# An mLSTM attention, a two-expert mixture and a dense layer in one kernel: where the steps of experts 0 and 1 stand, and when the second batch is routed

## The chip, the cores and the metric

One core of a Trainium2 chip. The metric is the device time of one execution in microseconds (us), the median over runs. The engines are TensorE (PE, matmuls; PEld is its weight loads), VectorE (DVE), ScalarE (ACT), GpSimd (POOL) and SyncE (SP, here the queue that issues most DMAs). Each engine takes its instructions in the order of the program; semaphores tie them together.

## The reference

Three layers follow each other. The attention is a recurrence over 768 tokens for 2 batches and 8 heads of 40; its output x (1536 tokens of 320 values) is routed to 2 of 8 experts, and the mixture's output goes through a dense layer with g = h cos h.

```python
h_tilde = np.einsum('bhde,bhe->bhd', C, qt)          # C, n: running states of the attention
y[:, :, t] = o * h_tilde / np.maximum(np.abs(nq), 1.0)
...
noisy_logits = x @ w_gate + np.log1p(np.exp(x @ w_noise)) * noise
top2 = np.argpartition(-noisy_logits, 2, axis=1)[:, :2]
...
h = np.maximum(x[mask] @ w1[e], 0.0)
out[mask] += top2_w[mask, k, None] * (h @ w2[e])
...
h = x @ w_in
return (h * np.cos(h)) @ w_out
```

## The kernel before

**Attention.** The recurrence is worked in chunks of 128 tokens, 6 per batch, so chunks n = 0 to 11; `att_step(n)` issues one. A chunk has its scores (`mm_s`), decay weights on ACT and POOL (`mk_w`), the product of both on DVE (`mk_p`, tile ppt), the scaled queries (`mk_q`, tile qtt, on POOL or DVE by a list of n), the running state (`mm_state`, `mk_state`, tile st), the output matmuls (`mm_out`, L306 and L310, tile pS) and the normalized rows (`mk_y`: an Abs on ACT, L321, and four DVE instructions, L322 to L327, that end in xt, called x(n) here). x(n) is written to DRAM (xd) by SP, transposed on PE (`rt_a`, L346), copied on ACT (L348), multiplied with the gating weights (`rt_b`, L355) and copied again (L359, tile Lt).

**Routing.** When a batch's six chunks are done, `router_a0` to `router_d` turn the gate values into lists of token indices: three small ACT instructions, then DVE work from L398 to L519 with two small products on PE (`router_b`, L441 to L444, and `router_c`, L504). `gather` (L546, on POOL) then fetches the rows of x of one group from DRAM into xgt.

**Experts.** Ten groups are worked: experts 0 and 1 on batch 0 (groups 0 and 1, up to 240 tokens each), experts 2 to 7 on both batches (up to 448), and experts 0 and 1 on batch 1. Each group has 8 steps of 128 hidden units; step k is step k mod 8 of group k // 8. Before its first step the gathered rows are transposed on PE and split on ACT and DVE into a high and a low part (`prep_slot`: L555, L557, L558, tiles xh and xl). `expert_step` first issues `split(k + 2)`, which cuts the weights of a later step into wh (a copy on ACT, L585) and wl (a subtraction, L587, on POOL, or on DVE in the two-slot groups for the k that L586 names), then the first product `mm1` (L594, 8 matmuls into pS), a Relu on ACT (L646, hb) and the low part on DVE (L649), and last the second product of the step before (`mm2`, L599 to L603, 6 matmuls into pA). The third matmul of mm1 is the first that reads wl. In this kernel steps of groups 0 and 1 have odd wl on DVE but for k in `POOL_SPLIT`, and 12 and 14 too.

**Order.** It is written out by hand. `manual_schedule` keeps the order in which the Python code issues, on each engine. Tables hold what is issued at which place: `mid[n]` and `fill[n]` inside `att_step(n)`, `put(n, ...)` behind it; after the attention the same `put(k, ...)` counts expert steps. `K0` is the first step of the main loop. Before, steps 0 to 3 are issued within chunks 10 and 11 and step 4 behind chunk 11; the second batch's routing then goes on behind steps 5 to 12, and the gathers of group 2 behind steps 10 and 11. From step 71 on the dense layer's steps follow (`moe2_step`), while its weights are converted on DVE between.

Of the kernel before, what the change touches and what calls it, by code (L numbers as in the profile page):

```python
# [15 lines left out]
OP = mybir.AluOpType  # L16
# [5 lines left out]
NC = S // C  # L22
# [18 lines left out]
def tile_mlstm_moe_moe2(ctx, tc, qk, kv, og, gi, gf, wcat, noise, wm1, wm2, cst, out):  # L41
    nc = tc.nc
    V, A, G, T, Y = nc.vector, nc.scalar, nc.gpsimd, nc.tensor, nc.sync
# [188 lines left out]
    def mk_q(n):  # L232
        if n >= 2 * NC or n % NC == 0:
            return
        d = L[n]
        d["qt"] = ap_.tile([128, NH, C], FT, name="qtt", bufs=2)
        (G if n in (1, 4, 5, 6, 7, 8, 9, 11) else V).tensor_tensor(out=d["qt"], in0=d["qk"][:, 2], in1=d["ge"], op=OP.mult)

    def mm_s(n, ws=range(NH)):
        if n >= 2 * NC:  # L240
            return
        d = L[n]
        for i in ws:
# [55 lines left out]
    def mm_out(n, between=None):  # L299
        c = n % NC  # L300
        d = L[n]
        p = d["po"] = psS()
        so = STS[(n + 1) % 2]
        for w in range(NH):
            if c:
                T.matmul(p[:, 82 * w:82 * w + 82], d["qt"][:, w, :], so[:, w, :], start=True, stop=False,  # L306
                         skip_group_check=True)
            for s in range(2):
                h = 2 * w + s
                T.matmul(twice(p, h), d["p"][:, h, :], d["v"][:, h:h + 1, :].to_broadcast([128, 2, 41]),  # L310
                         start=(not c), stop=bool(s) or not c, skip_group_check=True)
            if between and w < NH - 2:
                between(w)
# [221 lines left out]
    groups = [(e, T2, 2 * e) for e in (0, 1)]  # L535
# [37 lines left out]
        prep_x(d["xg"][i], groups[g][1][i], d["xh"], d["xl"], 128 * i, ps_)  # L573

    SP = {}
    POOL_SPLIT = (1, 7, 9, 11, 65, 67, 75)

    def split(k):
        g, f = divmod(k, 8)
        if g >= NG:  # L580
            return
        raw = WB[groups[g][0]]
        wh = mp.tile([128, FW], FR, name="wh", tag="wh", bufs=4)
        wl = mp.tile([128, FW], FR, name="wl", tag="wl", bufs=4)
        A.activation(wh, raw[:, f, :], AF.Copy)  # L585
        eng = V if len(groups[g][1]) == 2 and (k % 2 and k not in POOL_SPLIT or k in (12, 14)) else G  # L586
        eng.tensor_tensor(out=wl, in0=raw[:, f, :], in1=wh.bitcast(FT), op=OP.subtract)  # L587
        SP[k] = (wh, wl)

# [264 lines left out]
    def att_step(n):  # L854
        if n == 0:
            loads(0)
        if n:
            mk_e(n + 1)
        for f, a in pre.pop(n, []):
            f(*a)  # L860
        mm_state(n)
        if n:
            mm_s(n + 2, (0,))
        mm_out(n, (lambda w: mm_s(n + 2, (w + 1,))) if n else None)
        if n == 0:
            gates_t(2, 4)
        if n:
            rt_a(n - 1, psS if n == 7 else None)
        mm_s(n + 2, (3,) if n else range(NH))
        for f, a in mid.pop(n, []):  # L870
            f(*a)
        if n:
            rt_b(n - 1, psS if n == 9 else None)
        if n == 2:
            gates_t(4, NC)
        mk_state(n)
        mk_p(n + 1)
        mk_q(n + 1)
        mk_decay(n + 1)
        if n == 0:  # L880
            gates_c(2, 4)
        if n == 2:
            gates_c(4, NC)
        if n == 1:
            gates_a(4, NC)
        loads(n + 1)
        if n == 2 * NC - 1:
            mk_y(n)
        for f, a in fill.pop(n, []):
            f(*a)  # L890
        if n < 2 * NC - 1:
            mk_y(n)
        mk_w(n + 2)
        if n == 0:
            V.tensor_copy(tri, cc_[:, 0:128])
            V.tensor_copy(rb[:, 0], row0)
            V.memset(ones, 1.0)
            V.memset(os_[:, NC], 0.0)
        if n == 1:
            gates_b(4, NC)  # L900
        if n == 10:
# [15 lines left out]
    for i in range(8):  # L917
        put((6, 7, 8, 8, 8, 9, 9, 9)[i], load_w, 0, i, 1)
    put(10, load_w, 1, 0, 2)
    put(11, load_w, 1, 2, 2)  # L920
    put(11, load_w, 1, 4, 2)
    mid[6] = [(A.preload_act_table_set, ("natural_log_exp_and_others",))]
    fill[6] = [(router_a0, (0,))]
    put(6, router_a1, 0)
# [3 lines left out]
    fill[8] = [(router_b1, (0, 0))]  # L928
    put(8, router_b1, 0, 1)
    put(8, router_s)  # L930
    put(9, split, 1)
    mid[9] = [(router_c, (0,))]
    fill[9] = [(router_d, (0,)), (gather, (0, 0)), (gather, (0, 1)), (split, (0,))]
    put(9, router_a3, 0)
    put(10, router_a4, 0)
    mid[10] = [(prep_slot, (0, 0, psA)), (prep_slot, (0, 1, psA))]
    fill[10] = [(step, (0,))]
    put(10, step, 1)
    mid[11] = [(step, (2,))]
    put(11, step, 3)  # L940
    for i in range(2):
        put(10, gather, 1, i)
    K0 = 5
    for n in range(2 * NC):
        att_step(n)
        for f, a in at.pop(n, []):
            f(*a)
    rt_a(2 * NC - 1)
    step(4)
    rt_b(2 * NC - 1)  # L950
    router_a0(1)
    router_a1(1)
    att.close()
    wp = ctx.enter_context(tc.tile_pool(name="wp", bufs=1, reuse_waits="tile"))

    put(5, load_w, 1, 6, 2)
    put(5, router_a2, 1)
    put(5, prep_slot, 1, 0, psA)
    put(6, prep_slot, 1, 1, psA)
    put(6, router_b, 1)  # L960
    put(7, router_b1, 1, 0)
    put(7, router_b1, 1, 1)
    put(8, router_b2, 1)
    put(9, router_p, 1)
    put(10, router_c, 1)
    put(10, router_d, 1)
    put(11, router_a3, 1)
    put(12, router_a4, 1)
    for i in range(4):
        put(10 + i // 2, gather, 2, i)  # L970
        put((13, 14, 15, 15)[i], prep_slot, 2, i, (psA, psM)[i % 2])
    for g in range(2, NG - 1):
        n = len(groups[g + 1][1])
        for i in range(n):
# [20 lines left out]
    for f in range(12):  # L995
        k = 18 + (15 * f) // 4
# [166 lines left out]
```

## Time and profile before

| | |
|---|---|
| device time, three runs | 522.0, 523.95, 525.42 us (median 523.95) |
| span of the profiled execution, first to last instruction | 520.4 us |
| PE busy in the span | 489.0 us, 94% |
| PE weight loads, DVE, ACT, POOL busy | 468.5, 368.6, 326.0, 274.5 us |
| chain that ended last | PE 74%, DVE 13%, ACT 4%, DMA 4%, issue 3% |

The page gives no other time of the profiled execution than its span. The profile's lists of instructions in order of time ("timeline") give, for one engine, start, duration, line, operation and tiles; in brackets stands how long the engine was idle before, and what released it. "x3" is three instructions merged. The lists by stretch ("windows") give an engine's busy time within a part of the span. Times in the text are microseconds from the span's start.

### The profile page before, as it was taken

Reading aid. Unit: us, or ns where it says so; the run is one execution under the profiler, and the core shown is the slowest. Engines: PE = TensorE matmul, PEld = TensorE weight load, DVE = VectorE, ACT = ScalarE, POOL = GpSimd, SP = SyncE. Lnnn points to the kernel's source line nnn. Section 1 sums busy time; section 2 is a strip of 40 time slices with the busy share of each in tenths; the row PEclk is TensorE's granted clock in tenths of the full one; section 3 lists DMA queues with packets and bytes.
Section 4 is the critical chain, followed back from the end, with each engine's and each line's share of the span. In section 5 each row is a group of like instructions: output and inputs, shape, how many; then the busy total and the mean of one; then the engine's idle time right before and its main releaser. Section 6 shows DMA issues by size and latency. Waiting matters only on the chain.

```text
span 520.4 us, 9011 instructions
## 1 busy us (share of the span) xinstructions
PE 489.0 (94%) x3198; PEld 468.5 (90%) x3198; DVE 368.6 (71%) x779; ACT 326.0 (63%) x695; POOL 274.5 (53%) x234
## 2 busy tenths in 40 slices
PE   4899997799999999999999997999999999999995
PEld 3788886799999999999999997899999999999995
DVE  8874496568468776878776678788956655687773
ACT  3657866356555455545455475578877777777773
POOL 6435466556856868595868687264356347300000
PEclk9999999799999999999999999999999999999999
DMA  6889885386373918291938284130021003001001
GB/s 185 240 268 268 269 282 174 111 287 242 114 286 115 349 65 298 110 362 39 348 130 274 97 332 145 33 112 14 1 64 52 1 1 102 13 2 38 1 2 43
DMA packets 25396, 76.36 MB, mean 147 GB/s; under 512 B 3872, under 2 KB 11392, under 8 KB 25344
## 3 DMA queue, kind: packets, MB, share of 16 engines
q1 hardware_dynamic: 22752, 67.11, 37.2%
q0 software_dynamic: 2592, 8.61, 5.6%
q8 instruction: 27, 0.44, 0.3%
q14 instruction: 25, 0.20, 0.1%
HBM read 66.47 MB, written 9.22 MB: 145 GB/s over the span
## 4 chain that ended last, share of the span: by engine, by line
PE 74%; DVE 13%; ACT 4%; DMA 4%; issue 3%; SPq 0%; POOL 0%; DVEq 0%; ACTq 0%; POOLq 0%
PE pS L594 34%; PE pA L603 10%; PE pA L600 10%; PE pA L599 10%; PE pM L555 2%; PE pS L310 1%; PE pA L612 1%; PE pA L611 1%; ACT wt L209 1%; DMA xgt<-xd,idxe 1%; PE pM L355 1%; DMA gb<-gd 1%; DVE c_t L717 1%; DVE ppt L256 1%; DVE r_am L483 1%
## 5 line engine op out<-in xcount | busy, mean ns | idle before, releaser
L587 POOL TENSOR_TENSOR wl<-wraw,wh 128x704 fp32r<-128x704 f32 x69 | 122.9, 1790 | 61.6 <-ACT wh L585 55.7
L649 DVE SCALAR_TENSOR_TENSOR hb<-pS,hb 128x384 fp32r<-128x384 f32 (+2 forms) x128 | 45.9, 390 | 45.6 <-ACT hb L646 44.9
L585 ACT ACTIVATE wh<-wraw 128x704 fp32r<-128x704 f32 x80 | 62.9, 786 | 14.3 <-PE pA L611 7.3
L594 PE MATMUL pS<-xh,wh 128*128 128x448 f32 (+1 forms) x240 | 69.9, 346 | 0.5 <-ACT xh L557 0.5
L594 PE MATMUL pS<-xh,w 128*128 128x384 f32 x288 | 66.7, 340 | 1.6 <-DVE m_t L758 1.6
L594 PE MATMUL pS<-xh,wl 128*128 128x448 f32 (+1 forms) x240 | 66.5, 332 | 0.4 <-POOL wl L587 0.4
L599 PE MATMUL pA<-wh,hb 128*128 128x320 f32 x208 | 62.3, 309 | 0.0
L600 PE MATMUL pA<-wl,hb 128*128 128x320 f32 x208 | 62.2, 309 | 0.0
L743 ACT ACTIVATE m_t<-pS,magic 128x384 f32<-128x384 f32 x64 | 37.0, 579 | 28.7 <-PE pS L594 23.8
L646 ACT ACTIVATE hb<-pS 128x448 fp32r<-128x448 f32 (+1 forms) x80 | 37.7, 471 | 26.2 <-PE pS L594 18.5
L594 PEld LDWEIGHTS pS<-xh,w 128*128 128x128 f32 x288 | 50.0, 188 | 2.9 <-DVE m_t L758 2.9
L758 DVE SCALAR_TENSOR_TENSOR m_t<-m_t,pS 128x384 f32<-128x384 f32 x64 | 35.4, 553 | 16.7 <-ACT m_t L757 14.6
L603 PE MATMUL pA<-wh,hb 128*128 128x320 f32 x208 | 44.1, 312 | 3.0 <-DVE hb L649 2.9
L594 PEld LDWEIGHTS pS<-xh,wl 128*128 128x128 f32 x240 | 43.5, 192 | 2.7 <-POOL wl L587 0.5
L594 PEld LDWEIGHTS pS<-xh,wh 128*128 128x128 f32 x240 | 41.1, 192 | 1.5 <-ACT xh L557 0.6
L744 DVE TENSOR_SCALAR m_t<-m_t 128x384 f32<-128x384 f32 x64 | 23.1, 360 | 27.3 <-ACT m_t L743 27.0
L764 POOL TENSOR_TENSOR wl<-m_t,wh 128x384 fp32r<-128x384 f32 x25 | 25.4, 1016 | 30.7 <-ACT wh L762 21.4
L594 PE MATMUL pS<-xl,wh 128*128 128x448 f32 (+1 forms) x160 | 39.7, 329 | 0.0
L600 PEld LDWEIGHTS pA<-wl,hb 128*128 128x128 f32 x208 | 38.7, 186 | 0.6
L599 PEld LDWEIGHTS pA<-wh,hb 128*128 128x128 f32 x208 | 38.6, 186 | 0.6
L546 POOL DMA_INDIRECT xgt<-xd,idx x28 | 34.4, 1228 | 7.8 <-DVE idx L519 3.2
L745 DVE SCALAR_TENSOR_TENSOR m_t<-pS,m_t 128x384 f32<-128x384 f32 x64 | 35.7, 558 | 2.2
(201 smaller groups left out, 1239.7 us busy)
## 6 DMA issues: line engine op xcount, KB each, us to landing
wraw<-wm SPq DMA_DIRECT2D x36, 704.0 KB
raw<-wm SPq DMA_DIRECT2D x16, 704.0 KB
qk<-qk SPq DMA_DIRECT2D x24, 240.0 KB
gb<-gd SPq DMA_DIRECT2D x10, 512.0 KB
kv<-kv SPq DMA_DIRECT2D x12, 324.0 KB
yd<-yt SPq DMA_DIRECT2D x22, 160.0 KB
wraw<-wm SPq DMA_DIRECT2D x8, 352.0 KB
ogt<-og SPq DMA_DIRECT2D x6, 320.0 KB
```

Of the source, the lines that this page charges most:

```text
L546: G.indirect_dma_start(out=t[:n, :], out_offset=None, in_=XD[0:S, :] if g < 2 else XD[:, :], in_offset=bass.IndirectOffsetOnAxis(ap=(idxe ...
L585: A.activation(wh, raw[:, f, :], AF.Copy)
L587: eng.tensor_tensor(out=wl, in0=raw[:, f, :], in1=wh.bitcast(FT), op=OP.subtract)
L594: T.matmul(p[:, :n], w[:, 128 * k:128 * k + 128], x[:, m, :], start=(i == 0), stop=(i == 7))
L599: T.matmul(a[:n, :DM], hh[:, s], wh[:, KW:], start=first, stop=False)
L600: T.matmul(a[:n, :DM], hh[:, s], wl[:, KW:], start=False, stop=False)
L603: T.matmul(a[:n, :DM], hl[:, s], wh[:, KW:], start=False, stop=last)
L646: A.activation(hh[:, :n], p[:, :n], AF.Relu)
L649: V.scalar_tensor_tensor(out=hb[:, o:o + z - a], in0=p[:, a:z], scalar=0.0, in1=hh[:, a:z].bitcast(FT), op0=OP.max, op1=OP.subtract)
L743: A.activation(t, m["p"], AF.Identity, bias=magic, scale=0.5 / PI)
L745: V.scalar_tensor_tensor(out=t, in0=m["p"], scalar=0.5 / PI, in1=t, op0=OP.mult, op1=OP.subtract)
L758: V.scalar_tensor_tensor(out=s, in0=s, scalar=1.0, in1=m["p"], op0=OP.subtract, op1=OP.mult)
```

## The change

Steps 0 to 3 and the transposes of group 0 (`prep_slot`) are no longer issued within chunks 10 and 11. The two transposes stand at the end of chunk 11, steps 0 and 1 behind it, and the main loop starts with step 2. Splits 0 and 1 are issued behind chunk 10. In chunk 10, `mk_y` stands ahead of the next chunk's `mk_q` and `mk_p`, and the transposes of x(10) stand ahead of chunk 11's output matmuls. qtt of chunk 11 is made on DVE. Among the splits, 12 and 14 are POOL's again and 3 too, while 9 and 11 become DVE's. The second batch's routing is spread over steps 0 to 7 and not 4 to 10, and the gathers of group 2 stand behind steps 7 and 8, not 10 and 11. The last load of expert 1 is issued behind chunk 11.

```diff
--- before.py
+++ after.py
@@ -234,7 +234,7 @@
             return
         d = L[n]
         d["qt"] = ap_.tile([128, NH, C], FT, name="qtt", bufs=2)
-        (G if n in (1, 4, 5, 6, 7, 8, 9, 11) else V).tensor_tensor(out=d["qt"], in0=d["qk"][:, 2], in1=d["ge"], op=OP.mult)
+        (G if n in (1, 4, 5, 6, 7, 8, 9) else V).tensor_tensor(out=d["qt"], in0=d["qk"][:, 2], in1=d["ge"], op=OP.mult)
 
     def mm_s(n, ws=range(NH)):
         if n >= 2 * NC:
@@ -573,7 +573,7 @@
         prep_x(d["xg"][i], groups[g][1][i], d["xh"], d["xl"], 128 * i, ps_)
 
     SP = {}
-    POOL_SPLIT = (1, 7, 9, 11, 65, 67, 75)
+    POOL_SPLIT = (1, 3, 7, 65, 67, 75)
 
     def split(k):
         g, f = divmod(k, 8)
@@ -583,7 +583,7 @@
         wh = mp.tile([128, FW], FR, name="wh", tag="wh", bufs=4)
         wl = mp.tile([128, FW], FR, name="wl", tag="wl", bufs=4)
         A.activation(wh, raw[:, f, :], AF.Copy)
-        eng = V if len(groups[g][1]) == 2 and (k % 2 and k not in POOL_SPLIT or k in (12, 14)) else G
+        eng = V if len(groups[g][1]) == 2 and k % 2 and k not in POOL_SPLIT else G
         eng.tensor_tensor(out=wl, in0=raw[:, f, :], in1=wh.bitcast(FT), op=OP.subtract)
         SP[k] = (wh, wl)
 
@@ -861,10 +861,12 @@
         mm_state(n)
         if n:
             mm_s(n + 2, (0,))
+        if n == 2 * NC - 1:
+            rt_a(n - 1)
         mm_out(n, (lambda w: mm_s(n + 2, (w + 1,))) if n else None)
         if n == 0:
             gates_t(2, 4)
-        if n:
+        if 0 < n < 2 * NC - 1:
             rt_a(n - 1, psS if n == 7 else None)
         mm_s(n + 2, (3,) if n else range(NH))
         for f, a in mid.pop(n, []):
@@ -874,8 +876,13 @@
         if n == 2:
             gates_t(4, NC)
         mk_state(n)
-        mk_p(n + 1)
-        mk_q(n + 1)
+        if n == 2 * NC - 2:
+            mk_y(n)
+            mk_q(n + 1)
+            mk_p(n + 1)
+        else:
+            mk_p(n + 1)
+            mk_q(n + 1)
         mk_decay(n + 1)
         if n == 0:
             gates_c(2, 4)
@@ -888,7 +895,7 @@
             mk_y(n)
         for f, a in fill.pop(n, []):
             f(*a)
-        if n < 2 * NC - 1:
+        if n < 2 * NC - 2:
             mk_y(n)
         mk_w(n + 2)
         if n == 0:
@@ -917,8 +924,8 @@
     for i in range(8):
         put((6, 7, 8, 8, 8, 9, 9, 9)[i], load_w, 0, i, 1)
     put(10, load_w, 1, 0, 2)
-    put(11, load_w, 1, 2, 2)
-    put(11, load_w, 1, 4, 2)
+    for i in (2, 4, 6):
+        put(11, load_w, 1, i, 2)
     mid[6] = [(A.preload_act_table_set, ("natural_log_exp_and_others",))]
     fill[6] = [(router_a0, (0,))]
     put(6, router_a1, 0)
@@ -928,47 +935,44 @@
     fill[8] = [(router_b1, (0, 0))]
     put(8, router_b1, 0, 1)
     put(8, router_s)
-    put(9, split, 1)
     mid[9] = [(router_c, (0,))]
-    fill[9] = [(router_d, (0,)), (gather, (0, 0)), (gather, (0, 1)), (split, (0,))]
+    fill[9] = [(router_d, (0,)), (gather, (0, 0)), (gather, (0, 1))]
     put(9, router_a3, 0)
     put(10, router_a4, 0)
-    mid[10] = [(prep_slot, (0, 0, psA)), (prep_slot, (0, 1, psA))]
-    fill[10] = [(step, (0,))]
-    put(10, step, 1)
-    mid[11] = [(step, (2,))]
-    put(11, step, 3)
+    put(10, split, 0)
+    put(10, split, 1)
+    fill[11] = [(prep_slot, (0, 0, psA)), (prep_slot, (0, 1, psA))]
     for i in range(2):
-        put(10, gather, 1, i)
-    K0 = 5
+        put(11, gather, 1, i)
+    K0 = 2
     for n in range(2 * NC):
         att_step(n)
         for f, a in at.pop(n, []):
             f(*a)
     rt_a(2 * NC - 1)
-    step(4)
+    step(0)
     rt_b(2 * NC - 1)
     router_a0(1)
     router_a1(1)
+    step(1)
     att.close()
     wp = ctx.enter_context(tc.tile_pool(name="wp", bufs=1, reuse_waits="tile"))
 
-    put(5, load_w, 1, 6, 2)
-    put(5, router_a2, 1)
+    put(2, router_a2, 1)
+    put(3, router_b, 1)
+    put(4, router_b1, 1, 0)
+    put(5, router_b1, 1, 1)
     put(5, prep_slot, 1, 0, psA)
+    put(6, router_b2, 1)
     put(6, prep_slot, 1, 1, psA)
-    put(6, router_b, 1)
-    put(7, router_b1, 1, 0)
-    put(7, router_b1, 1, 1)
-    put(8, router_b2, 1)
-    put(9, router_p, 1)
-    put(10, router_c, 1)
-    put(10, router_d, 1)
-    put(11, router_a3, 1)
-    put(12, router_a4, 1)
+    put(7, router_p, 1)
+    put(7, router_c, 1)
+    put(7, router_d, 1)
+    put(9, router_a3, 1)
+    put(10, router_a4, 1)
     for i in range(4):
-        put(10 + i // 2, gather, 2, i)
-        put((13, 14, 15, 15)[i], prep_slot, 2, i, (psA, psM)[i % 2])
+        put(7 + i // 2, gather, 2, i)
+        put((12, 13, 14, 14)[i], prep_slot, 2, i, (psA, psM)[i % 2])
     for g in range(2, NG - 1):
         n = len(groups[g + 1][1])
         for i in range(n):
```

On PE, around chunk 11, the end of chunk 10's output matmuls, x(9)'s transposes and what follows them. Tiles: st and qtt feed the state's part of the output, ppt and kv the chunk's own part; xgt are gathered rows, wc the gating weights. Before:

```order
L310 MATMUL pS<-kv,ppt 128x82
L346 MATMUL pM<-ident,xt 128x128 x3
L555 MATMUL pA<-ident,xgt 128x128 x3
L555 MATMUL pA<-ident,xgt 128x112 x3
L355 MATMUL pM<-wc,xTt 128x128 x3
L594 MATMUL pS<-xh,wh 128x240 x2
L594 MATMUL pS<-xh,wl 128x240 x2
L594 MATMUL pS<-xl,wh 128x240 x2
```

and now:

```order
L310 MATMUL pS<-kv,ppt 128x82
L346 MATMUL pM<-ident,xt 128x128 x3
L355 MATMUL pM<-wc,xTt 128x128 x3
L346 MATMUL pM<-ident,xt 128x128 x3
L306 MATMUL pS<-st_99,qtt 128x82
L310 MATMUL pS<-kv,ppt 128x2x41 x2
L306 MATMUL pS<-st_99,qtt 128x82
L310 MATMUL pS<-kv,ppt 128x2x41 x2
```

The transposes of the gathered rows and the two steps behind them have left this place; chunk 11's output follows x(10)'s transposes directly.

On DVE, the same place in the change, from the last state update to chunk 11's products (den is the denominator, ogt the output gate):

```order
L293 TENSOR_TENSOR st_99<-pS,st_99 40x4x41 x2
L322 TENSOR_SCALAR den<-den 128x8
L323 RECIPROCAL den<-den 128x8
L324 SCALAR_TENSOR_TENSOR ogt<-ogt,den 128x320
L327 SCALAR_TENSOR_TENSOR xt<-pS,ogt 128x320
L237 TENSOR_TENSOR qtt<-qk_93,get 128x512
L256 TENSOR_TENSOR ppt<-pA,wt 128x512 x2
```

and before, from there to the products and x(10):

```order
L558 TENSOR_TENSOR xl<-pA,xh 128x2x112
L560 TENSOR_TENSOR xh<-pA,xh 64x112
L293 TENSOR_TENSOR st_99<-pS,st_99 40x4x41 x2
L256 TENSOR_TENSOR ppt<-pA,wt 128x512 x2
L649 SCALAR_TENSOR_TENSOR hb<-pS,hb 128x240
L322 TENSOR_SCALAR den<-den 128x8
```

x(10) has moved ahead of chunk 11's products, and qtt has come from POOL to stand between.

On POOL, at the gathers of group 2 (xgt<-xd,idx), with the splits (wl) around them. Before, the splits for steps 9, 10 and 11 (their names end in 1406, 1433 and 1465), four gathers, and the split for step 16 (1622):

```order
L587 TENSOR_TENSOR wl_1406<-wraw_1150,wh_1405 128x704
L587 TENSOR_TENSOR wl_1433<-wraw_1150,wh_1432 128x704
L587 TENSOR_TENSOR wl_1465<-wraw_1150,wh_1464 128x704
L546 DMA xgt_1532<-xd_103,idx_113 128x320
L546 DMA xgt_1534<-xd_103,idx_113 128x320
L546 DMA xgt_1561<-xd_103,idx_113 128x320
L546 DMA xgt_1563<-xd_103,idx_113 64x320
L587 TENSOR_TENSOR wl_1622<-wraw_1402,wh_1621 128x704
```

and now, from the splits for steps 7 and 8 (1345, 1377) over 10 and 12 (1463, 1522) to 14 (1569):

```order
L587 TENSOR_TENSOR wl_1345<-wraw_761,wh_1344 128x704
L587 TENSOR_TENSOR wl_1377<-wraw_1110,wh_1376 128x704
L546 DMA xgt_1456<-xd_103,idx_113 128x320
L546 DMA xgt_1458<-xd_103,idx_113 128x320
L587 TENSOR_TENSOR wl_1463<-wraw_1110,wh_1462 128x704
L546 DMA xgt_1490<-xd_103,idx_113 128x320
L546 DMA xgt_1492<-xd_103,idx_113 64x320
L587 TENSOR_TENSOR wl_1522<-wraw_1110,wh_1521 128x704
L587 TENSOR_TENSOR wl_1569<-wraw_1110,wh_1568 128x704
```

The splits for steps 10 and 12 have come to stand behind gathers that wait for the second batch's indices.

## Rows read from the trace of the kernel before

**Rows 1.** Windows: stretch, its length, busy of each engine, clock, DMA share, GB/s

```profile
80.00:100.00 20.00, 13.80 (x107) 12.90 (x106) 11.50 (x31) 10.02 (x26) 12.29 (x13) 0.83 0.43 142
...
120.00:140.00 20.00, 19.26 (x145) 17.95 (x144) 13.63 (x39) 11.58 (x24) 13.64 (x10) 1.00 0.37 127
140.00:160.00 20.00, 20.00 (x122) 19.08 (x121) 13.33 (x23) 10.73 (x18) 12.45 (x10) 1.00 0.74 275
```

**Rows 2.** Timeline of PE, chunk 10's output and the gathered rows

```profile
84.94 0.42 PE L306 MATMUL pS<-st,qtt 128*128 128x82 f32 x2 [0.76 <-DVE r_hi L513]
...
87.65 0.49 PE L346 MATMUL pM<-ident,xt 128*128 128x128 f32 x3
90.18 0.55 PE L555 MATMUL pA<-ident,xgt 128*128 128x128 f32 x3 [2.04 <-DMA xgt<-xd,idxe]
93.92 0.82 PE L555 MATMUL pA<-ident,xgt 112*128 112x112 f32 x3 [3.19 <-DMA xgt<-xd,idxe]
```

**Rows 3.** Windows of 2 us, columns as in rows 1; the third last is the clock

```profile
90.00:92.00 2.00, 0.55 (x3) 0.31 (x3) 0.70 (x2) 0.49 (x1) 2.00 (x4) 0.90 1.04 408
92.00:94.00 2.00, 0.08 (x1) 0.09 (x2) 0.02 (x1) 0.00 (x0) 2.00 (x2) 0.50 0.23 89
...
98.00:100.00 2.00, 2.00 (x16) 2.00 (x16) 1.71 (x5) 1.27 (x4) 1.84 (x2) 0.89 0.03 8
```

**Rows 4.** Timeline of DVE, chunk products, x(9), x(11), and the routing's ends

```profile
82.90 1.29 DVE L256 TENSOR_TENSOR ppt<-pA,wt 128x512 f32<-128x512 f32 x2
84.11 0.68 DVE L237 TENSOR_TENSOR qtt<-qk,get 128x512 f32<-128x512 f32 x1
...
85.23 0.16 DVE L322 TENSOR_SCALAR den<-den 128x8 f32<-128x8 f32 x1
...
86.19 0.49 DVE L327 SCALAR_TENSOR_TENSOR xt<-pS,ogt 128x320 f32<-128x320 f32 x1
...
107.19 0.49 DVE L327 SCALAR_TENSOR_TENSOR xt<-pS,ogt 128x320 f32<-128x320 f32 x1
...
111.75 0.21 DVE L398 SCALAR_TENSOR_TENSOR pM<-Lt,pM 128x48 f32<-128x48 f32 x1 [1.50 <-ACT pM L393]
...
124.59 0.18 DVE L519 TENSOR_SCALAR idx<-r_hi 128x32 uint32<-128x32 f32 x1
```

**Rows 5.** Timeline of PE, x(11)'s transposes and step 16's first matmul

```profile
107.83 0.52 PE L346 MATMUL pM<-ident,xt 128*128 128x128 f32 x3 [0.71 <-DVE xt L327]
...
134.50 0.68 PE L594 MATMUL pS<-xh,wh 128*128 128x448 f32 x2 [0.47 <-ACT xh L557]
```

**Rows 6.** Timeline of ACT, an earlier chunk's copy of x and its Abs

```profile
74.94 0.49 ACT L348 ACTIVATE xTt<-pM 128x384 f32<-128x384 f32 x1 [1.83 <-PE pM L346]
...
76.53 0.17 ACT L321 ACTIVATE den<-pS 128x8 f32<-128x8 f32 x1
```

**Rows 7.** Timeline of POOL, first and last gather of group 2, a later split

```profile
125.05 1.37 POOL L546 DMA_INDIRECT xgt<-xd,idx  x1 [3.19 <-DVE idx L519]
...
129.22 0.99 POOL L546 DMA_INDIRECT xgt<-xd,idx  x1 [0.30 <-PE pA L600]
...
138.40 1.71 POOL L587 TENSOR_TENSOR wl<-wraw,wh 128x704 fp32r<-128x704 f32 x1 [0.36 <-ACT wh L585]
```

**Rows 8.** Line 587 on DVE (min, median, max ns); timelines of POOL and DVE

```profile
L587 DVE TENSOR_TENSOR wl<-wraw,wh x11: 877/884/1498, 100.6 to 327.3; 128x704 fp32r<-128x704 f32 x11
...
326.37 1.72 POOL L587 TENSOR_TENSOR wl<-wraw,wh 128x704 fp32r<-128x704 f32 x1 [3.48 <-ACT wh L585]
...
327.34 1.50 DVE L587 TENSOR_TENSOR wl<-wraw,wh 128x704 fp32r<-128x704 f32 x1 [0.34 <-ACT wh L585]
```

**Rows 9.** Chain of waits, 84 to 136 us: start, length, what

```profile
96.05 2.99 PE pS L594 x16
...
125.61 0.90 PE pS L594 x8
...
127.38 0.90 PE pS L594 x8
```

## The prediction

> **What bounds the kernel now.** I read the busy time by stretches first. From 140 us TensorE (PE) is busy 20.00 of 20 us, and from 120 to 140 us 19.26 of 20; the gap is in 80:100, where it is busy 13.80 us at a mean granted clock of 0.83 [rows 1]. So only what lies between about 84 us and the first step of the third group (step 16, whose first matmul starts at 134.50 [rows 5]) can become shorter; right behind it PE is full, and whatever step 16 gains or loses, the end gains or loses. I measure the change by the time at which step 16 starts.
>
> PE's own timeline then shows what the gap is. Chunk 10's output matmuls run from 84.94 us, the transposes of x(9) end at 88.14, and then PE stands before the two transposes of gathered rows (L555), first 2.04 us, then 3.19 us, for the gather [rows 2]. They stand in PE's row ahead of everything left of the attention. The clock falls from 2.4 GHz late in 90:92 (mean 0.90), is at 0.50, its lower level of 1.2 GHz, in 92:94, and is back by 98:100 (mean 0.89) [rows 3]. Sixteen matmuls of two steps took 2.99 us there, where eight take 0.90 us at full clock [rows 9].
>
> Last I read the other three engines. The last chunk's x(11), from which the second batch's routing starts, is ready on VectorE (DVE) at 107.19 + 0.49 = 107.68 us. The routing chain starts on DVE at 111.75 (L398) and ends with the indices at 124.59 + 0.18 = 124.77 us (L519) [rows 4]: 13.02 us, with hardly an idle moment on DVE between. GpSimd (POOL) starts the four gathers of group 2 at 125.05 and ends them at 130.21, 1.29 us each; a split of weights takes it 1.7 us [rows 7].
>
> **The change, part by part.** *Attention.* Steps 0 to 3 and the two transposes leave PE's row ahead of chunk 11; the gather is hidden behind the chunk. What is left there is one chain through three engines, with PE waiting. From 88.14: from the start of x(9)'s copy on ScalarE (ACT) to the end of the next denominator's Abs is 74.94 to 76.70, 1.76 us [rows 6], so 90.0 with a small hand-over. Denominator to x takes 85.23 to 86.68, 1.45 us [rows 4]: x(10) at 91.45. Its product qtt(11), moved from POOL to DVE, takes 0.68 us and the two ppt 1.29 us [rows 4].
>
> Now the hidden price of moving it. The splits 0 and 1 on POOL (1.7 us each [rows 7]) now stand at the same moment: the first begins about 90.8 and ends about 92.5. In the trace a DVE instruction with both inputs in SBUF that meets such a split doesn't run beside it: DVE's split at 327.34 took 1.50 us where the median of the 11 is 0.88, and ended 0.75 us after POOL's of 326.37 to 328.09 [rows 8]. qtt at 84.11 met nothing. The Trainium skill, "SBUF — State Buffer", section "SBUF: two separate sides", states this as a rule: a GpSimd operation and a VectorE one with two SBUF inputs exclude each other for a whole instruction. By it qtt(11) waits for the split; by qtt's own row it costs 0.68 us and x(11) comes 1.1 us earlier. I take the wait, because of rows 8: qtt(11) ends at 93.25, the first ppt at 93.9, and chunk 11's output matmuls, 84.94 to 87.65 or 2.71 us [rows 2], of which the first 0.2 need only qtt, end at 96.4. A gating product, copy and Abs (1.2 us) and 1.45 us for x follow: x(11) at 99.1, 8.6 us earlier than before.
>
> *PE behind x(11).* Steps 0 to 3 must now be done here. A plain step is 1.77 us, 0.90 of it the first product (mm1), 0.87 the second (mm2) [rows 9]. Before, four mm1 and three mm2 were done by 107.83, when x(11) was transposed [rows 5]: 4 x 0.90 + 3 x 0.87 = 6.2 us come in. The waits around the last two transposes of group 2, about 1.3 us of the time ahead of 134.50, go, since these stand a step earlier now. Of the 26.67 us from 107.83 to 134.50, 12 mm1 and 12 mm2 are 21.24; the other 5.4 are routing products, transposes and waits, and without the 1.3 us some 4 us of small work, the same work at other places in the change. Without any other wait step 16 would start at 134.5 - 8.6 + 6.2 - 1.3 = 130.8 us; counted up from 99.1 with 16 mm1, 15 mm2 and 4 us of small work it is 130.6. I take 130.5: a gain of 4.0 us.
>
> *Routing and POOL.* This gain is lost again. L398 starts 4.07 us after x(11) before; one mm1 stands between now instead of a whole step, so 102.3. The 13.02 us on DVE held one split of weights, now it is two, those for steps 5 and 9 (0.9 us more [rows 8]); the copy of a result, 0.4 us, goes behind. Steps of 1.77 us pace the parts, which I price at 1.1 us of short waits, plus 0.5 us for a DVE split meeting POOL's: an estimate from rows 8 and 9. Indices at about 102.3 + 15.1 = 117.4. That is bounded below by 13.0 (115.3) and above by 17 (119.3).
>
> Before, the split for step 10 was done ahead of the gathers on POOL, and 12 and 14 were DVE's. Now POOL's row is two gathers, split 10, two gathers, split 12. In order on one engine: 117.4 + 0.28 + 2 x 1.29 + 0.36 + 1.7 [rows 7] = 122.3 for split 10. PE wants it at 99.3 + 2.4 (small work) + 10 x 0.90 + 9 x 0.87 + 0.2 = 118.7, two matmuls into mm1 of step 10. It waits 3.6 us. Everything of PE stands behind it. Then 2 x 1.29 + 0.15 + 0.36 + 1.7 = 4.8 us later, at 127.1, split 12; PE gets there 3.5 us after its restart, at 125.8, and waits 1.3 us more. These two waits, 4.9 us, take all of the gain.
>
> *What is hidden.* The loads of experts 1 and 2 are issued in the same order on SP, and the DMA engines are busy for 0.43 and 0.37 of 80:100 and 120:140 [rows 1]. The early splits 0 and 1 are wanted only at 99.8, ready by 95. Gathers of group 1 land some 10 us before use. SP's longer wait for x(11) is over earlier than before. Nothing there is on the path; if a load were late, it would cost at most its own 2 or 3 us.
>
> **Sum.** 130.5 + 4.9 = 135.4, against 134.5: +0.9 us, bounded by -4.0 (POOL in time) and about +3 (indices at 119.3). The span would be 521.3. The page's span is 520.4; the median of the runs, 523.95, lies 3.55 us above it, and I let that stay. So 523.95 + 0.9, rounded to 525.0 us: no change that a measurement of this kernel could tell, which needs about 1% (5.2 us).
>
> **The rivals.** *POOL in time.* If the routing on DVE runs with less waiting than I priced, or PE is later at step 10 for other reasons, the 4.9 us go. For it: before, PE waited only for tenths between 108 and 133 us although DVE was full. Against it: step 7's end alone fixes the last routing product at about 114.5, and two gathers and a split need 4.9 us more, so split 10 can't be there before 119.8. Even then about 1.1 us is lost. Time: 523.95 - 4.0 + 0.5 = 520.5, at the very best 519.5. Chance 0.16.
>
> *The clock falls in the attention's tail* (the slower side). Before, it fell late in 90:92, after PE had worked 0.55 us since 88.14, and rose in 98:100, with PE at work since 93.92 [rows 2, 3]. Now PE does about 0.9 us between 88.1 and 91.5 and then waits again until 93.9. If the clock falls there, chunk 11's output, the gating product and mm1 of step 0 take 2.99/1.80 = 1.66 times their time [rows 9]: (2.5 + 0.65 + 0.9) x 0.66 = 2.7 us, all on the chain to x(11) and from it: 525.0 + 2.7 = 527.7. If it falls again in the wait of 3.6 us at step 10, some 0.9 us more remain after the wait at step 12: 528.6; with late indices 530. The Trainium skill, "TensorE: Matmul & The Clock Gate", section "What's actually happening", says that the slow state is the default and activity releases it, which speaks for this rival; it decides if the clock falls ahead of chunk 11's matmuls. Chance 0.28.
>
> *DVE becomes the bound.* Seven steps' worth of routing, splits and results on one engine: if each meeting with a POOL split costs 0.75 us as in rows 8, and three or four occur, the indices come at 119.3 and step 16 at 137.3: 526.8. For it: rows 8. Against: most such pairs fall apart in time. Chance 0.11.
>
> **How the numbers follow.** Forecast 0.45 (its own range 523.5 to 526.5), rivals 0.16, 0.28, 0.11. The range 520.5 to 529.8 takes in the lower half of the first rival and nearly all of the second. Faster by over 1% (below 518.7) needs more than the first rival's best: 0.04. Slower by over 1% (above 529.2) needs the clock to fall twice or with late indices, a good third of the second rival and some of the third: 0.14. Within 1%: 0.82.
>
> **What would show it.** In the new profile: L398's start near 102 and L519's end near 117 (the routing); PE idle before L594 of step 10 with POOL's wl as releaser, 3 to 4 us, and about 1 us before step 12; qtt(11) on DVE longer than 0.68 us; PE without waits for xgt; clock 1.00 in 90:98 (else the second rival). I am wrong if PE has no wait for POOL near 119 us, or if x(11) isn't ready before 101 us.

## The result, and the profile after

| | before | after |
|---|---|---|
| device time, median of four runs each | 524.68 us (522.0 to 526.13) | 530.17 us (529.56 to 531.5) |
| ratio after to before, 95% interval | | 1.0121, 1.0094 to 1.0148 |
| span of the profiled execution | 520.4 us | 527.7 us |
| x(11) ready, from the start of chunk 10's qtt | 23.57 us | 17.85 us |
| step 16 starts, from the same point | 50.39 us | 56.13 us |

The change makes the kernel slower by 1.2%, where 525.0 us was forecast with a range up to 529.8. The last two rows need a common zero: both kernels are the same up to the start of chunk 10's qtt on DVE, 84.11 us before [rows 4] and 85.35 after, so after's trace is 1.24 us late before the change begins. From there step 16 is 5.74 us late. With the 1.24 that is 6.98 of the 7.3 us by which the spans differ; past step 16 nothing of size is left.

Busy time by stretches of after, to be held against [rows 1] (columns: PE, PEld, DVE, ACT, POOL busy, granted clock, DMA share, GB/s):

```profile
80.00:100.00 20.00, 15.80 (x113) 14.43 (x112) 12.94 (x33) 8.80 (x24) 11.73 (x13) 0.81 0.70 213
100.00:120.00 20.00, 18.64 (x142) 17.44 (x141) 14.75 (x57) 12.34 (x28) 10.23 (x6) 0.93 0.49 172
120.00:140.00 20.00, 15.49 (x125) 14.59 (x126) 14.58 (x28) 8.92 (x21) 10.82 (x8) 1.00 0.41 151
140.00:160.00 20.00, 20.00 (x124) 19.37 (x124) 10.36 (x23) 10.31 (x17) 14.29 (x11) 1.00 0.60 226
```

Two losses stand out. PE is busier in 80:100 than before (15.80 against 13.80 us), but at a granted clock of 0.81, and 100:120 is at 0.93 too. And 120:140, nearly full before (19.26 of 20 us), has 4.5 us of idle PE. The same in stretches of 2 us, as in [rows 3]:

```profile
90.00:92.00 2.00, 0.94 (x6) 0.74 (x6) 0.65 (x3) 0.98 (x4) 1.15 (x2) 1.00 0.86 286
92.00:94.00 2.00, 0.87 (x3) 0.50 (x3) 1.91 (x3) 0.83 (x3) 1.86 (x2) 0.59 1.00 388
98.00:100.00 2.00, 2.00 (x11) 2.00 (x11) 0.00 (x0) 0.00 (x0) 0.27 (x1) 0.50 0.79 317
102.00:104.00 2.00, 1.21 (x10) 0.90 (x9) 1.83 (x6) 0.98 (x3) 0.00 (x0) 0.85 0.05 19
104.00:106.00 2.00, 2.00 (x17) 1.80 (x17) 0.94 (x3) 1.69 (x4) 0.79 (x1) 1.00 0.83 228
```

The clock falls from 2.4 to 1.2 GHz inside 92:94, after PE had little to do from 90 on, and comes back in 102:104. PE's own list in order of time (start, duration, line; in brackets the idle time before, and what ended it) shows what ran in that stretch, and every wait from x(11) to step 16:

```profile
92.94 0.87 PE L346 MATMUL pM<-ident,xt 128*128 128x128 f32 x3 [1.99 <-DVE xt L327]
94.42 0.72 PE L306 MATMUL pS<-st,qtt 128*128 128x82 f32 x2 [0.60 <-DMA wraw<-wm]
99.80 1.56 PE L355 MATMUL pM<-wc,xTt 128*128 128x128 f32 x6
101.16 1.41 PE L555 MATMUL pA<-ident,xgt 128*128 128x128 f32 x6
103.35 0.52 PE L346 MATMUL pM<-ident,xt 128*128 128x128 f32 x3 [0.79 <-DVE xt L327]
...
121.33 0.52 PE L504 MATMUL pM<-r_bm,r_am 128*128 128x64 bf16 x12 [1.80 <-DVE r_fl L468]
126.78 0.49 PE L594 MATMUL pS<-xh,wl 128*128 128x240 f32 x2 [1.08 <-POOL wl L587]
131.30 0.49 PE L594 MATMUL pS<-xh,wl 128*128 128x240 f32 x2 [0.69 <-POOL wl L587]
134.24 0.56 PE L603 MATMUL pA<-wh,hb 128*128 128x320 f32 x2 [1.41 <-DVE hb L649]
141.48 0.57 PE L594 MATMUL pS<-xh,wh 128*128 128x448 f32 x2
```

Chunk 11's output matmuls take from 94.42 to 99.80, 5.38 us, where chunk 10's took 2.71 [rows 2]. The DMA named at 94.42 had nothing to do with L306: qtt(11) ended on DVE at 94.37. The transposes of gathered rows (101.16) no longer wait. Behind x(11) there are four waits, 1.80 + 1.08 + 0.69 + 1.41 = 4.98 us, for the routing on DVE, for POOL's splits of steps 10 and 12, and for hb. DVE and POOL in the same places:

```profile
92.31 0.49 DVE L327 SCALAR_TENSOR_TENSOR xt<-pS,ogt 128x320 f32<-128x320 f32 x1
92.72 1.65 DVE L237 TENSOR_TENSOR qtt<-qk,get 128x512 f32<-128x512 f32 x1
102.71 0.49 DVE L327 SCALAR_TENSOR_TENSOR xt<-pS,ogt 128x320 f32<-128x320 f32 x1
106.73 0.21 DVE L398 SCALAR_TENSOR_TENSOR pM<-Lt,pM 128x48 f32<-128x48 f32 x1 [0.77 <-ACT pM L393]
122.34 0.18 DVE L519 TENSOR_SCALAR idx<-r_hi 128x32 uint32<-128x32 f32 x1
124.75 2.74 DVE L587 TENSOR_TENSOR wl<-wraw,wh 128x704 fp32r<-128x704 f32 x1 [0.51 <-ACT wh L585]
129.41 1.87 DVE L432 TENSOR_SCALAR r_w<-r_w 128x6 f32<-128x6 f32 x1
131.54 1.52 DVE L434 TENSOR_TENSOR r_w<-r_w 128x6 f32<-128x6 f32 x1
```

```profile
92.14 3.76 POOL L587 TENSOR_TENSOR wl<-wraw,wh 128x704 fp32r<-128x704 f32 x2 [0.99 <-ACT wh L585]
122.79 0.97 POOL L546 DMA_INDIRECT xgt<-xd,idx  x1 [4.12 <-DVE idx L519]
125.02 1.70 POOL L587 TENSOR_TENSOR wl<-wraw,wh 128x704 fp32r<-128x704 f32 x1
129.54 3.50 POOL L587 TENSOR_TENSOR wl<-wraw,wh 128x704 fp32r<-128x704 f32 x2
```

Beside these splits of POOL four DVE instructions are long: qtt(11) 1.65 for 0.68 us beside 92.14, a split 2.74 for 0.88 beside 125.02, and L432 and L434, which work on 128x6 values and take 0.16 and 0.17 us where nothing meets them (at 95.29 and 95.71 in e9's trace), 1.87 and 1.52 beside 129.54. They read and write SBUF alone. Not every DVE instruction is held: while POOL works at two splits from 107.47 to 110.85, the routing's searches (L405, L407) and a result that reads PSUM (L649) run at their usual length there, L405 0.51 us as in e1, where POOL has nothing to do then. The last two of the four hold up hb, for which PE waits 1.41 us.

### The profile page after: what moved, and what is told of

The parts are those of the page before. It is cut to its first block, busy times and chain, and to the rows that moved or that the text cites. A ratio compares the mean times of both kernels' runs of the same rounds, so it can differ in the third digit from the quotient of the medians.

```text
span 527.7 us, 9013 instructions
## 1 busy us (share of the span) xinstructions
PE 493.3 (93%) x3198; PEld 471.1 (89%) x3198; DVE 373.7 (71%) x779; ACT 326.2 (62%) x695; POOL 275.3 (52%) x234
## 4 chain that ended last, share of the span: by engine, by line
PE 74%; DVE 12%; DMA 6%; issue 4%; ACT 3%; POOL 1%; SPq 1%; DVEq 0%; ACTq 0%; POOLq 0%
PE pS L594 34%; PE pA L603 10%; PE pA L600 10%; PE pA L599 10%; DMA qk<-qk 2%; PE pM L555 2%; PE pS L310 2%; DMA gb<-gd 1%; PE pA L612 1%; PE pA L611 1%; DMA wraw<-wm 1%; PE pA L247 1%; PE pM L355 1%; DVE c_t L717 1%; DVE ppt L256 1%
## 5 line engine op out<-in xcount | busy, mean ns | idle before, releaser
L587 POOL TENSOR_TENSOR wl<-wraw,wh 128x704 fp32r<-128x704 f32 x70 | 125.1, 1797 | 65.6 <-ACT wh L585 57.9
L649 DVE SCALAR_TENSOR_TENSOR hb<-pS,hb 128x384 fp32r<-128x384 f32 (+2 forms) x128 | 45.8, 390 | 47.7 <-ACT hb L646 47.0
L599 PEld LDWEIGHTS pA<-wh,hb 128*128 128x128 f32 x208 | 38.6, 186 | 0.6
L603 PEld LDWEIGHTS pA<-wh,hb 128*128 128x128 f32 x208 | 33.2, 186 | 5.7 <-DVE hb L649 5.7
```

Source lines behind the costliest of these rows:

```text
L599: T.matmul(a[:n, :DM], hh[:, s], wh[:, KW:], start=first, stop=False)
L603: T.matmul(a[:n, :DM], hl[:, s], wh[:, KW:], start=False, stop=last)
L649: V.scalar_tensor_tensor(out=hb[:, o:o + z - a], in0=p[:, a:z], scalar=0.0, in1=hh[:, a:z].bitcast(FT), op0=OP.max, op1=OP.subtract)
```

## The experiments

Each is compared with the kernel before on its own chip. x(11) and step 16 are counted, as above, from the start of chunk 10's qtt in its own trace.

| run | ratio to before, 95% interval | x(11) | step 16 |
|---|---|---|---|
| before | 1 | 23.57 | 50.39 |
| after | 1.0121 (1.0094 to 1.0148) | 17.85 | 56.13 |
| e1_attention_half | 1.0076 (1.0053 to 1.0099) | 17.85 | 56.06 |
| e2_filled_tail | 1.0075 (1.0045 to 1.0104) | 14.91 | 53.19 |
| e3_late_splits_on_dve | 1.0008 (0.9986 to 1.0029) | 17.84 | 51.20 |
| e4_qtt_on_pool | 1.0110 (1.0082 to 1.0138) | 18.70 | 56.98 |
| e5_fill_and_late_dve | 0.9938 (0.9914 to 0.9962) | 14.90 | 48.25 |
| e6_before_filled | 0.9967 (0.9947 to 0.9987) | 22.30 | 49.10 |
| e7_weights_later | 1.0089 (1.0069 to 1.0109) | 17.85 | 55.96 |
| e8_attention_half_filled | 0.9933 (0.9913 to 0.9952) | 14.91 | 48.18 |
| e9_first_splits_on_dve | 1.0111 (1.0080 to 1.0143) | 16.76 | 55.25 |
| e10_all_three | 0.9962 (0.9940 to 0.9983) | 14.45 | 47.80 |
| e11_attention_half_clean | 1.0031 (1.0014 to 1.0049) | 17.86 | 51.35 |

**The clock.** e2 adds five matmuls to after whose product nobody reads, two and three of them where PE waits in the attention's tail:

```diff
+    def warm(n):
+        p = psA()
+        for i in range(n):
+            T.matmul(p[:, 0:320], ident, cc_[:, 0:320], start=True, stop=True)
...
         if n == 2 * NC - 1:
             rt_a(n - 1)
+            warm(2)
...
             rt_b(n - 1, psS if n == 9 else None)
+        if n == 2 * NC - 2:
+            warm(3)
```

> The changed kernel with five matmuls of 320 columns more on TensorE in the attention's tail, whose result nobody reads (three behind x(9)'s gating product, two behind x(10)'s transposes), so that PE works where it waited. Theory A (the low clock costs 2.7 us of the chain): clock 1.00 throughout the tail, x(11) near 100.3 us and not 103.2, 527.4 us. Theory B (the chain is bound by ACT and DVE and the clock costs nothing, or doesn't depend on PE's work here): 530 us or up to 0.5 us more.

```profile
92.00:94.00 2.00, 1.85 (x10) 1.14 (x9) 2.00 (x3) 0.49 (x1) 2.00 (x2) 1.00 0.89 291
98.00:100.00 2.00, 0.79 (x7) 0.80 (x7) 1.86 (x5) 0.60 (x3) 0.00 (x0) 1.00 0.88 351
```

```profile
99.21 0.52 PE L346 MATMUL pM<-ident,xt 128*128 128x128 f32 x3 [1.37 <-DVE xt L327]
117.19 0.52 PE L504 MATMUL pM<-r_bm,r_am 128*128 128x64 bf16 x12 [1.79 <-DVE r_fl L468]
122.65 0.49 PE L594 MATMUL pS<-xh,wl 128*128 128x240 f32 x2 [1.08 <-POOL wl L587]
127.17 0.49 PE L594 MATMUL pS<-xh,wl 128*128 128x240 f32 x2 [0.69 <-POOL wl L587]
130.11 0.57 PE L603 MATMUL pA<-wh,hb 128*128 128x320 f32 x2 [1.41 <-DVE hb L649]
```

These are e2's stretches of 2 us and its PE. With PE at work the clock is 1.00 throughout; x(11) and step 16 both come 2.94 us earlier, and the same four waits stand behind x(11), to a hundredth. So the clock costs after 2.9 us, and the waits have nothing to do with it. The price of such a fall is not a constant, though: in e7, which is the same program up to there and has x(11) at the same place, the clock comes back only at 106 us of its trace (104:106 at 0.50, 106:108 at 1.00). Counted from the zero, the end of step 0's second product comes 4.4 us later there than in e2; in after it is 3.0.

**The waits behind the routing.** e3 gives the splits 10, 12 and 14 back to DVE, and split 9 to POOL:

```diff
-    POOL_SPLIT = (1, 3, 7, 65, 67, 75)
+    POOL_SPLIT = (1, 3, 7, 9, 65, 67, 75)
-        eng = V if len(groups[g][1]) == 2 and k % 2 and k not in POOL_SPLIT else G
+        eng = V if len(groups[g][1]) == 2 and (k % 2 and k not in POOL_SPLIT or k in (10, 12, 14)) else G
```

> The changed kernel with the splits for steps 10, 12 and 14 on DVE and the one for step 9 on POOL ahead of the gathers: no split on POOL meets a DVE instruction behind the gathers. Theory A (POOL's splits behind the gathers, by being late and by holding DVE's instructions, cost the waits at steps 10 to 12): those three waits (1.08, 0.69, 1.41 us) go, and 0.9 us of the 1.80 us before the last routing product: 4.1 us, 526.1 us. Theory B (DVE is simply full): three more splits there cost as much as they save, 529 to 531 us.

In e3's list of PE one wait is left between x(11) and step 16:

```profile
120.48 0.52 PE L504 MATMUL pM<-r_bm,r_am 128*128 128x64 bf16 x12 [0.87 <-DVE r_fl L468]
136.63 0.57 PE L594 MATMUL pS<-xh,wh 128*128 128x448 f32 x2
```

Step 16 comes 4.93 us earlier with x(11) where it was, 0.8 more than theory A's 4.1, which had counted PE's idle time alone. A wait costs more than that: in after, step 10's third pair of matmuls starts 1.79 us behind its first, in e3 0.44, so 1.35 us more for a wait of 1.08. PE's busy time from x(11)'s transposes to step 16 is 33.05 us in after and 32.22 in e3, for the same steps. The wait at L504 is 0.93 us shorter because the routing on DVE has one split less to carry (from x(11) to the end of the indices 18.4 us, in after 19.3).

e7 leaves the splits and only moves the small weight instructions (L427 to L434) out of POOL's way:

```diff
-    put(9, router_a3, 1)
-    put(10, router_a4, 1)
+    put(13, router_a3, 1)
+    put(14, router_a4, 1)
```

> The changed kernel, with the second batch's weights of the mixture (L427 to L434) behind steps 13 and 14 and not 9 and 10, so that these small DVE instructions meet no split on POOL. It tells apart whether PE's last wait (1.41 us for hb) comes from POOL's hold on DVE or from DVE's own queue of splits. Theory A, the hold: L432 and L434 take 0.15 and 0.17 us and not 1.87 and 1.52, the wait for hb goes, the waits of 1.80, 1.08 and 0.69 stay, step 16 starts 1.4 us earlier: about 528.8 us, ratio 1.009. Theory B, DVE's own work: a wait of 1 us or more stays there, 530 us.

The wait for hb is gone, as theory A says. But the hold has only moved: L432 and L434 still take 1.19 and 1.40 us, now beside splits of POOL from 137.81, against what was expected, and PE waits inside step 16 for an xl that stands behind them on DVE:

```profile
142.21 0.67 PE L594 MATMUL pS<-xl,wh 128*128 128x448 f32 x2 [1.15 <-DVE xl L558]
```

So the start of step 16, 0.17 us earlier than in after, hides this loss: step 17 starts 1.24 us later than in after. PE has 1.79 us left at L504 and 0.49 for a split of POOL. The clock adds to it: since it comes back later in the tail, L504 starts 1.42 us later, and it falls again behind the wait there, which it did not in after's trace:

```profile
120.00:122.00 2.00, 0.46 (x13) 0.46 (x14) 1.61 (x5) 0.63 (x1) 0.00 (x0) 1.00 0.81 197
122.00:124.00 2.00, 2.00 (x16) 2.00 (x14) 0.97 (x4) 0.37 (x1) 0.97 (x1) 0.77 0.99 386
124.00:126.00 2.00, 2.00 (x10) 2.00 (x10) 1.04 (x2) 1.12 (x2) 1.69 (x2) 0.50 1.00 418
126.00:128.00 2.00, 2.00 (x16) 2.00 (x15) 2.00 (x2) 1.01 (x2) 1.84 (x2) 0.88 0.92 348
```

In time e7 (1.0089) can't be told from after with certainty. It settles what the wait was for, not what it is worth.

**qtt(11).** Two ways to take it from beside POOL's splits: e4 gives it back to POOL, e9 moves the splits 0 and 1 to DVE, behind ppt(11).

```diff
-        (G if n in (1, 4, 5, 6, 7, 8, 9) else V).tensor_tensor(out=d["qt"], in0=d["qk"][:, 2], in1=d["ge"], op=OP.mult)
+        (G if n in (1, 4, 5, 6, 7, 8, 9, 11) else V).tensor_tensor(out=d["qt"], in0=d["qk"][:, 2], in1=d["ge"], op=OP.mult)
```

> The changed kernel with chunk 11's qtt on POOL again, where it stands ahead of the splits 0 and 1. Theory A (the meeting of qtt on DVE with the split on POOL, 1.65 us instead of 0.68, is on the chain to x(11)): qtt ends near 92.4 and not 94.3 us, x(11) about 1.0 to 1.5 us earlier, 529.0 us. Theory B (DVE's instruction for x(10) meets POOL's qtt instead, and as much is lost there): 530 us.

```profile
92.10 1.13 DVE L322 TENSOR_SCALAR den<-den 128x8 f32<-128x8 f32 x1 [2.69 <-ACT den L321]
93.50 1.68 DVE L324 SCALAR_TENSOR_TENSOR ogt<-ogt,den 128x320 f32<-128x320 f32 x1
```

That is e4's DVE: POOL has qtt at 91.94 for 1.26 us and the splits from 93.17, and now the instructions of x(10) are held, 1.13 and 1.68 us for 0.17 and 0.49. x(11) is 0.85 us later than in after: theory B. In either order it was DVE's instruction that was held.

```diff
+        if k < 2:
+            eng = V
         eng.tensor_tensor(out=wl, in0=raw[:, f, :], in1=wh.bitcast(FT), op=OP.subtract)
```

> The changed kernel, with the splits 0 and 1 on DVE behind ppt(11), and not on POOL beside qtt(11). Theory A, POOL's split holds qtt(11) for 1.0 us: qtt(11) takes 0.68 us and not 1.65, output matmuls of chunk 11 start 1.0 us earlier, step 16 1.0 us earlier: about 529.0 us, ratio 1.010. If PE's shorter wait keeps the clock up, up to 2.9 us more go: 526. Theory B, qtt(11) took 1.65 us for another reason: nothing changes, 530 us.

In e9 qtt(11) takes 0.68 us and x(11) comes 1.09 us earlier, step 16 0.88: theory A for the hold. The 0.1% in the ratio is less than the runs can tell. The clock falls all the same, only later (0.76 in 94:96, 0.53 still in 100:102).

**The halves of the change.** e1 puts routing, gathers and the splits' engines back to before's places and keeps the attention half (the first ones shown; the others likewise):

```diff
-    POOL_SPLIT = (1, 3, 7, 65, 67, 75)
+    POOL_SPLIT = (1, 7, 9, 11, 65, 67, 75)
-    put(2, router_a2, 1)
-    put(3, router_b, 1)
+    put(5, router_a2, 1)
+    put(6, router_b, 1)
```

> The changed kernel with its attention half alone: the second batch's routing, its gathers and the splits' engines stand again at the steps of the kernel before. Theory A (two separate losses: the low clock in the attention's tail, and waits of the routing half behind x(11)): the waits of 1.80, 1.08, 0.69 and 1.41 us behind x(11) go, 5.0 us, and about 0.8 us of wait at the last transposes of group 2 comes back: 530.2 - 4.2 = 526.0 us, with the clock still at 0.50 near 94 to 102 us. Theory B (the tail alone is the loss, the waits behind x(11) would only move to other places): 529 to 530 us.

It was no clean half (527.63 us where 526.0 was expected). Split 3 on DVE met POOL's split 2 (2.22 us at 109.16), PE waited 2.27 us for hb behind it, and the clock, which had come back late as in e7 (0.54 in 104:106), fell a second time (0.50 in 114:116). So 1.0076 is not what the half is worth. e11 is e1 with split 3 on POOL, `POOL_SPLIT = (1, 3, 7, 9, 11, 65, 67, 75)`; e8 is e11 with the five idle matmuls of e2.

> The attention half alone (routing, gathers and splits at the places of before), now at full clock (five idle matmuls) and with split 3 on POOL, so that neither the clock nor a held split blurs it. Theory A, the move of the steps is worth 2 to 3 us once the clock is paid for, and the lower steps for the routing bring nothing: x(11) 14.9 us behind the start of chunk 10's qtt, step 16 48.3 or earlier (before: 50.4), 521.3 us or less, ratio 0.996 or less. Theory B, the routing needs the lower steps: PE waits for gathered rows at the transposes of group 2, step 16 at 49.5 or later, 522.6 us or more.

> The attention half alone with split 3 on POOL, and without idle matmuls: what the first half of the change is worth as it stands, with the clock falling in the tail. Theory A, the sum is attention -2.2 us (as with idle matmuls), clock +2.9 us, routing half +5.0 us: step 16 at 51.1 us behind the start of chunk 10's qtt (before: 50.4), 0.7 us more than before, about 524.5 us, ratio 1.001. Theory B, the attention half makes most of the loss by itself, clock or not: step 16 at 53 or later, 526.5 us or more, ratio 1.005 or more.

```profile
99.83 0.52 PE L346 MATMUL pM<-ident,xt 128*128 128x128 f32 x3 [1.37 <-DVE xt L327]
121.28 0.56 PE L603 MATMUL pA<-wh,hb 128*128 128x320 f32 x2 [0.26 <-DVE hb L649]
132.95 0.68 PE L594 MATMUL pS<-xh,wh 128*128 128x448 f32 x2 [0.47 <-ACT xh L557]
```

In e8's list of PE only 0.26 and 0.47 us of waits are left between x(11) and step 16, with the routing where it was before. Step 16 starts at 48.18, as early as in e5 with the lower steps (48.25). The two also differ in the engines of the splits 10 and 11, so this is no clean pair, but it shows that the lower steps aren't needed for that time. e11 gives 51.35 and 1.0031: the attention half as it stands costs 1.0 us in its trace, e8's -2.2 and 3.2 for the clock, and the routing half with its splits adds 56.13 - 51.35 = 4.8 us.

**Sums.** e5 is e2 and e3 together, e10 is e5 and e9 together.

> The changed kernel with both earlier edits: five idle matmuls in the attention's tail (2.9 us of clock) and the splits 10, 12 and 14 on DVE (4.9 us of waits behind the routing). Theory A, the two losses are separate terms that add: x(11) 14.9 us behind the start of chunk 10's qtt, step 16 48.3 us behind it (before: 50.4), so 2.1 us less than before, about 521.4 us, ratio 0.996. Theory B, they are one loss seen twice (an earlier x(11) only makes PE wait longer for the second batch's indices, or the other way round): step 16 not earlier than in the better of the two, 51.2 us, and about 524 us, ratio 1.000 or more.

> The changed kernel with all three edits: idle matmuls, late splits on DVE, first two splits on DVE. If the three terms add (2.9, 4.9 and 1.0 us): step 16 47.3 us behind the start of chunk 10's qtt, 3.1 us less than before, about 520.4 us, ratio 0.994. If the routing on DVE (15.1 us or more from x(11)) is the bound by then: step 16 at 48.3 or later, 521.5 us or more.

In e5 step 16 comes 7.88 us earlier than in after; 2.94 + 4.93 is 7.87. The two losses are separate. e10 gains 0.45 us more in its trace (47.80, between the 47.3 and the 48.3 that were expected), but its time is not below e5's (the intervals overlap), so the first splits on DVE are worth nothing that was measured.

**The kernel before, filled.** e6 puts such idle matmuls, 3 and 5, ahead of before's two waits for gathered rows.

```diff
-    mid[10] = [(prep_slot, (0, 0, psA)), (prep_slot, (0, 1, psA))]
+    mid[10] = [(warm, (3,)), (prep_slot, (0, 0, psA)), (warm, (5,)), (prep_slot, (0, 1, psA))]
```

> The kernel before, with idle matmuls (3 and 5) in front of the two transposes that wait for the gather, so that PE isn't idle there. Theory A, the kernel before pays for the clock too, in the steps behind the gather (94.5 to 98.5 us at 1.2 GHz): clock 1.00 through 90:100, the two steps end 2.0 us earlier, step 16 2.0 us earlier, about 521.5 us, ratio 0.996. Theory B, chunk 11's qtt and ppt are what x(11) waits for there: the clock is up and nothing comes of it, 523.5 us, ratio 1.000.

The clock is 1.00 there and step 16 comes 1.29 us earlier, less than the 2.0 expected; PE has a new wait of 0.22 us there, for chunk 11's state, which explains only a part. So before paid for its clock too, but less than half of what after does. Both e5 and e8 beat before by 0.6 to 0.7%, and e8 leaves the routing where it was. Against e6 the move of the steps itself is worth 49.10 - 48.18 = 0.9 us in the traces.

## Why the prediction was wrong

**The attention's chain: right, but for the clock.** x(11) was worked out at 99.1 us, 15.0 from the zero of the table; without the fall of the clock it is at 14.91 (e2, e8). The hidden price in it, POOL's split holding qtt(11) for 1.1 us, is there: 1.65 us for 0.68, and 1.09 us when e9 takes it away. The Trainium skill's rule of an exclusive lock, "SBUF — State Buffer", section "SBUF: two separate sides" (a GpSimd instruction and a VectorE one with two SBUF inputs exclude each other, and whichever starts first has the shared ports for its whole instruction), agrees with these rows: POOL's split starts at 92.14, qtt(11) at 92.72. That the earlier one goes first does not show in all rows of after: DVE's split at 124.75 and L432 at 129.41 start ahead of POOL's splits of 125.02 and 129.54, in the last moments of a gather on POOL, and are held all the same. Why is not shown.

**The choice between forecast and second rival: the first step that failed.** The forecast took the clock as staying up in the tail, with 0.45, and gave its fall 0.28. The clock fell ahead of chunk 11's matmuls, which is the point the rival named, and cost 2.94 us where 2.7 was priced. The evidence was at hand: in [rows 2, 3] the clock fell after PE had worked 0.55 us since 88.14, and the prediction itself found about 0.9 us of work between 88.1 and 91.5 and another wait behind it. PE's plan for the tail was little fuller than the stretch that had lost the clock before. The prediction had set x(11) ready before 101 us as its test: it came at 103.20, 101.96 on before's scale. A loss of over 1% was thought to need a second fall or late indices; it came with one fall, and with indices that, less the 2.94 us, stand at 118.3 on before's scale, inside the bounds. The Trainium skill, "TensorE: Matmul & The Clock Gate", section "What's actually happening", has the slow state as the default that activity releases, and e2, where nothing but activity was added, agrees.

**The steps that come in behind x(11): the second failed step.** Forecast were +6.2 us for four first and three second products, -1.3 for waits at the last transposes, and 0.3 of rounding down. The stretch from x(11)'s transpose to step 16, as PE's busy time, before, in after and in e8:

```profile
107.83:134.50 26.67, 25.91 (x216) 24.67 (x216) 20.41 (x74) 17.06 (x38) 17.83 (x12) 1.00 0.64 230
```

```profile
103.35:141.48 38.13, 33.05 (x265) 31.26 (x266) 29.20 (x84) 21.21 (x45) 21.91 (x15) 1.00 0.45 161
```

```profile
99.83:132.95 33.12, 32.28 (x265) 31.05 (x265) 22.99 (x81) 21.71 (x46) 22.94 (x15) 1.00 0.55 187
```

The steps cost 32.28 - 25.91 = 6.4 us in e8 and 6.3 in e3, near the 6.2 that were priced; of the 7.1 in after, 0.8 belong to the waits, since they go with them in e3. The term that failed is the -1.3: before, PE stood idle for 26.67 - 25.91 = 0.76 us in the whole stretch, so at least 0.5 us of these waits were never idle time. The gain of 4.0 us that the forecast began with is 2.2 in e8, where these transposes stand as before, and 2.1 in e5, where they stand a step earlier and nothing waits for them; there 0.87 us of wait at L504 have come in instead.

**The waits for POOL: right in sum by luck, wrong in place.** Priced were 3.6 us at step 10 and 1.3 at step 12, 4.9 in all; measured were 4.98 us of idle time, but only 1.08 + 0.69 = 1.77 of them for POOL's splits. PE lost its first 1.80 us a stage earlier, at L504, where the routing's own product stands in its row; so it came later to step 10 and waited 1.08 there, and 0.69 at step 12. That the sum agrees is luck: the chain from the routing to POOL cost 1.80 + 1.77 = 3.57 us of idle time, less than priced, and the last 1.41 us belong to the third rival, whose mechanism the forecast had put at 0.5 us: POOL's splits holding DVE. The routing took 15.79 us from L398 to the indices, 15.1 were forecast.

**The sum.** Forecast for step 16 was 135.4 us; after, on before's scale, gives 84.11 + 56.13 = 140.24. Of the 4.8 us between, 2.9 are the clock, 1.3 the saving that wasn't there, 0.3 the rounding, 0.1 the steps (6.3 for 6.2) and 0.2 the waits. These cost 5.1 us more than before's, where 4.9 were priced: PE's idle time in the stretch grew from 0.76 to 38.13 - 33.05 = 5.1 us, by 4.3, and 0.8 us are the longer busy time beside them. That the gain would be eaten by waits was right in kind; the range was too narrow by 0.4 us on the slow side.

## What to carry to other kernels

Before filling or opening a gap, add up what PE will do in the new one: if it is as empty as a stretch of the old trace that lost its clock, price the matmuls behind it at the lower level. An edit that moves small DVE work next to long GpSimd operations has to be priced by POOL's durations, not by its own, and it helps to choose the engine of each split by what DVE does at that moment. A term that says "these waits go" has to be held against the idle time of that stretch, which one row of busy time gives: here 0.76 us against a term of 1.3. It is no sharp bound, since in e3 4.1 us of idle time less were worth 4.9.

## What was not expected of the hardware

Even a TENSOR_SCALAR, with one input, on 128x6 or 128x8 values is held for the length of a POOL split or product (L432 1.87 us, L322 1.13 us, for 0.16 and 0.17). A RECIPROCAL of the same size is not (L323 0.20 us at 93.27 in e4, beside POOL's split from 93.17). [rows 8] had shown the hold for splits alone, but before's trace has it for small instructions too: L322 takes 0.69 us at 105.65, beside POOL's split of 104.60 to 106.30. After a wait of 1.8 us at L504 the clock stayed at 1.00 in after and e2, but fell in e7 and e9 behind a wait of 1.79 us; what decides that was not settled, and neither was why it came back later in e7 and e1 than in after.
